# One store of 127 rows issued as two stores, of 112 and of 15 rows, in a fused attention, gating and Fourier kernel on Trainium2

## The chip, the cores and the metric

The kernel runs on one core of one Trainium2 chip. The metric is the device time of one execution in microseconds (us); of several runs the median is given. TensorE is called PE below, VectorE DVE, ScalarE ACT, GpSimd POOL and SyncE SP. SP computes nothing here: it is the queue from which almost all DMAs are issued, in program order.

## The reference

Three stages run one after the other, for a batch of 4, a sequence of 576 and a width of 512:

```python
# 1: attention in a window of 64 positions, 8 heads of 64
attn = softmax(where(0 <= i - j < 64, q @ k.T / 8, -1e9)) @ v
# 2: gated unit with a spatial mix
h = relu(x @ w_in); u, v = h[..., :512], h[..., 512:]
x = (u * (w_spatial @ layernorm(v) + b_spatial)) @ w_out
# 3: Fourier mix and channel MLP
u = x + real(fft(fft(x, axis=1), axis=2))
out = u + relu(layernorm(u) @ w_ch1) @ w_ch2
```

The change touches the end of the Fourier mix, where `u` of stage 3 is written to memory.

## The kernel before

Stages 1 and 2 and the Fourier mix run batch by batch (b = 0 to 3). Stage 3's channel MLP runs after them over all 2304 rows in five chunks of 384 or 512 rows (`TILES`, `GROUPS`). Numbers of 32 bits are split into a high and a low part, and a product is three matmuls (`PASS`).

The order of the work is written out by hand. A string for each batch (`ORDER`, lines 38 to 46) names the next step by a letter, and every engine runs its instructions in the order in which the steps issued them. While batch b goes through stage 2 and the Fourier mix (letters i and u, the `items` of line 675), the attention of batch b + 1 is woven in (letters s, q, v: attention step, load of q and k, load of v). In batch 3 there is no attention left; there the weights of the channel MLP are loaded and decoded (letter n) and the first chunk is loaded back and normalized (letters c and d). SP is one queue: a load that stands behind a store in the program is issued behind it.

The Fourier mix of a batch uses the symmetry of a real transform. `e2(b, mt)` (line 621) makes three tiles, mt = 0, 1 and 2. For mt = 0 and 1 it makes two tiles of `u`, r = 0 with rows in natural order and r = 1 with mirrored rows, and for mt = 2 one tile of 65 rows. A tile is written by DVE (lines 655 to 661) and finished by POOL (line 662), and then SP stores it to the scratch tensor `u_scr` in memory (lines 664 to 670). For mt = 0 and r = 1 row 0 would repeat a row that is already there, so only rows 1 to 127 are stored: 127 rows of 2 KB each. So each batch has one store of 128 rows (line 666), one of 127 (line 668), one of 128 (line 666), one of 128 (line 670) and one of 65 (line 664), in this order on SP, and the kernel has the 127-row store four times, at 147.7, 243.4, 332.2 and 417.3 us.

What stands behind these stores:

- In batch 0, SP next loads v for the attention (line 350). POOL shifts a copy of it (lines 355 and 356), and behind that on POOL stand the `norm_rstd` steps (lines 484 and 485) of the gating of batch 1.
- In batch 2, SP next loads two tiles `uu` of the first chunk back from `u_scr` (`load_u`, line 742) and then raw weights (line 218). DVE takes the statistics of the first tile (line 478), and behind that on DVE stand the normalizations (line 489) of the gating of batch 3. ACT splits their results (line 205), and then evacuates the `ps_u` results (line 533) that PE waits for before its next `ps_v` matmuls (line 500).
- In batch 3, the tile `u` of mt = 2 takes the buffer of an earlier tile `u` (the pool `tr` has five buffers), so DVE's line 655 waits until the store of that tile has landed. Behind it on DVE stands line 792, which makes the low part of the first hidden tile, and PE's second-layer matmuls (line 812) wait for that.

Of the kernel before, what the change touches and what calls it, by code (L numbers as in the profile page):

```python
# [111 lines left out]
def tile_kernel(ctx: ExitStack, tc: tile.TileContext, q, k, v, w_in, w_sp, b_sp, w_out, w_c1, w_c2,  # L112
                rows, ident, mask, t1h, t1l, s2c, s2s, out):
    nc = tc.nc
    act, dve, pool, pe, sp = nc.scalar, nc.vector, nc.gpsimd, nc.tensor, nc.sync
# [5 lines left out]
    def raw_tile(i):  # L121
        return st_p.tile([128, 512], I64, tag=f"st{i}", name="st")
# [16 lines left out]
    def psT(nm="psT"):  # L139
        return ps_t.tile([128, 512], F32, tag="t", name=nm)  # L140

    def psO(nm="psO"):
        return ps_o.tile([128, 512], F32, tag="o", name=nm)

    def tr(nm, shape=(128, 512), dt=F32):
        return tr_p.tile(list(shape), dt, tag="tr", name=nm)

    u_scr = dr_p.tile([B * S, DM], F32, name="u_scr")
# [472 lines left out]
    def e2(b, mt):  # L621
        rev, nat = REV[b], NAT[b] + mt * 128
        n = 128 if mt < 2 else 65
        cc = mt * 128
        xs = []
        for r in range(2 if mt < 2 else 1):
            px = psT("ps_xt")
            c0 = cc + 321 * r
            for m in range(4):
                pe.transpose(px[0:n, m * 128:(m + 1) * 128], FR[:, m, c0:c0 + n], idt)  # L630
            x = tr("x2h")
            act.activation(out=x[0:n], in_=px[0:n], func=AF.Copy, scale=0.5)
            xs.append(x)
        k = mt if b < B - 1 else 1 + mt
        if k < 2:
            room = raw_tile(k).bitcast(F32).rearrange("p (r d) -> p r d", r=2)
            room = [room[:, i] for i in range(2)]
        else:
            room = [tr("u") for _ in xs]
        pa, pb = psO("ps_a"), psO("ps_b")  # L640
        for ps, tb, c0, nn in ((pa, tc2, 0, NK2), (pb, ts2, 256, 256)):
            oc = slice(c0, c0 + nn)
            c = 0
            for kt in range(2):
                for w, a in PASS:
                    st = (2 * kt + w) * NM + cc
                    pe.matmul(ps[0:n, 0:nn], lhsT=tb[:, st:st + n], rhs=zz[:, kt, a, oc],
                              start=(c == 0), stop=False)
                    c += 1
            st = 4 * NM + cc  # L650
            pe.matmul(ps[0:n, 0:nn], lhsT=tb[0:99, st:st + n], rhs=zs[0:99, oc], start=False, stop=True)

        def row(r, x):
            u = room[r]
            dve.tensor_tensor(out=u[0:n, 0:257], in0=pa[0:n, 0:257], in1=x[0:n, 0:257], op=ALU.add)
            o = x[0:n, 257:512]
            if r == 0:
                dve.tensor_tensor(out=o, in0=o, in1=pb[0:n, 1:256], op=ALU.subtract)
            else:
                dve.tensor_tensor(out=o, in0=o, in1=pb[0:n, 1:256], op=ALU.add)  # L660
            dve.tensor_tensor(out=u[0:n, 511:256:-1], in0=u[0:n, 1:256], in1=o, op=ALU.subtract)
            pool.tensor_tensor(out=u[0:n, 1:256], in0=u[0:n, 1:256], in1=o, op=ALU.add)
            if mt == 2:
                sp.dma_start(out=u_scr[rev + 255:rev + 320, :], in_=u[0:65])
            elif r == 0:
                sp.dma_start(out=u_scr[nat:nat + 128, :], in_=u)
            elif mt == 0:
                sp.dma_start(out=u_scr[rev:rev + 127, :], in_=u[1:128])
            else:
                sp.dma_start(out=u_scr[rev + 127:rev + 255, :], in_=u)  # L670

        for r, x in enumerate(xs):
            row(r, x)
# [299 lines left out]
```

## Time and profile before

| what | value |
|---|---|
| time, median of 3 runs (lowest to highest) | 839.21 us (839.21 to 840.34) |
| time of the profiled execution | 839.83 us |
| its span in the trace | 838.0 us |
| mean granted clock of PE | 0.983 of full |
| PE busy (matmul) | 797.2 us, 95% of the span |
| DVE, ACT, POOL busy | 418.0, 316.0, 243.3 us |
| DMA on SP's queue | 55.23 MB, 23.6% of 16 engines over the span |

An engine's busy time is the time in which it ran instructions. The time around the span is 839.83 - 838.0 = 1.8 us. PE waits little as a whole; the waits that are left lie in few places, so single stretches have to be read and not the average.

### The profile page before, as it was taken

The numbers are of one execution on the slowest core, as the hardware profiler recorded it, in microseconds if no ns is written. First come the engines' busy times: TensorE is split into PE (matmuls) and PEld (weight loads), VectorE is DVE, ScalarE is ACT, GpSimd is POOL, SyncE is SP. The second block draws the span as 40 slices with busy tenths as digits, with TensorE's granted clock in tenths as the row PEclk, the third lists the DMA queues.
The fourth block names the chain that finished last, engine by engine and source line by source line (L and its number), as shares of the span: only waits on it lengthen the run. The fifth ranks groups of instructions, "written<-read, shape, count | busy, mean of one in ns | idle before, by whom it ended". The sixth has DMA issues, their size and how long they took to land.

```text
span 838.0 us, 13450 instructions
## 1 busy us (share of the span) xinstructions
PE 797.2 (95%) x4969; PEld 700.9 (84%) x4969; DVE 418.0 (50%) x1099; ACT 316.0 (38%) x939; POOL 243.3 (29%) x332
## 2 busy tenths in 40 slices
PE   6789999999999999797959999999999999999998
PEld 4678989889998999697959999988888888888886
DVE  3896766444463446376638888953212212231012
ACT  5877657365654554243413333321111111111100
POOL 2665552454224541345113333422000100000000
PEclk9999999999999999898979999999999999999999
DMA  8735433312222110423014444333000300011001
GB/s 202 176 84 171 126 102 93 99 33 60 54 61 68 31 26 16 142 81 97 14 44 151 128 126 139 110 93 122 13 13 14 101 12 26 14 51 50 1 1 50
DMA packets 89438, 62.71 MB, mean 75 GB/s; under 512 B 64859, under 2 KB 77403, under 8 KB 89373
## 3 DMA queue, kind: packets, MB, share of 16 engines
q1 hardware_dynamic: 87676, 55.23, 23.6%
q0 software_dynamic: 1696, 6.63, 2.3%
q8 instruction: 39, 0.64, 0.3%
q14 instruction: 27, 0.21, 0.1%
HBM read 52.40 MB, written 9.44 MB: 74 GB/s over the span
## 4 chain that ended last, share of the span: by engine, by line
PE 85%; DMA 5%; DVE 5%; issue 2%; POOL 1%; ACT 1%; SPq 1%; POOLq 0%; DVEq 0%; ACTq 0%
PE ps_y L812 24%; PE ps_h L788 24%; PE ps_v L500 6%; PE ps_d L558 6%; PE ps_u L530 5%; PE ps_c L543 5%; PE psS L389 3%; PE ps_x L443 3%; PE ps_pt L426 2%; PE ps_z L604 1%; DMA u_scr<-u 1%; DMA st<-in_moe_w_ch_dram 1%; PE ps_z L612 1%; DMA va<-in_v_dram 1%; PE ps_kn L366 1%
## 5 line engine op out<-in xcount | busy, mean ns | idle before, releaser
L812 PE MATMUL ps_y<-ar 128*128 128x512 f32 x756 | 184.1, 391 | 0.0
L812 PEld LDWEIGHTS ps_y<-ar 128*128 128x128 f32 x756 | 141.3, 188 | 28.2
L792 DVE SCALAR_TENSOR_TENSOR ar<-ps_h,ar 128x512 fp32r<-128x512 f32 (+1 forms) x80 | 50.9, 637 | 203.5 <-ACT ar L791 203.5
L791 ACT ACTIVATE ar<-ps_h 128x512 fp32r<-128x512 f32 (+1 forms) x80 | 44.4, 555 | 284.2 <-PE ps_h L788 284.2
L788 PE MATMUL ps_h<-ar 128*128 128x384 f32 (+1 forms) x672 | 147.9, 365 | 0.1
L788 PEld LDWEIGHTS ps_h<-ar 128*128 128x128 f32 x672 | 122.2, 188 | 16.8 <-issue 0.7
L207 POOL TENSOR_TENSOR ar<-dec,ar 128x512 fp32r<-128x512 f32 x36 | 49.7, 1382 | 69.0 <-ACT ar L205 68.7
L500 PE MATMUL ps_v<-ar 128*128 128x512 f32 (+1 forms) x240 | 61.1, 411 | 5.4 <-ACT uf L533 3.8
L402 ACT ACTIVATE P<-P,nm 128x128 f32<-128x128 f32 (+1 forms) x144 | 55.5, 386 | 17.1 <-DVE nm L396 12.3
L484 POOL TENSOR_SCALAR rs<-mv 128x1 f32<-128x1 f32 (+1 forms) x38 | 9.4, 247 | 180.6 <-DVE mv L479 180.2
L543 PE MATMUL ps_c<-ar 128*128 128x288 f32 x384 | 58.4, 302 | 1.2 <-DVE gf L548 1.2
L500 PEld LDWEIGHTS ps_v<-ar 128*128 128x128 f32 (+1 forms) x240 | 44.1, 187 | 18.3 <-ACT uf L533 4.1
L396 DVE CUSTOM_DVE_ANT_0 P<-psS,msk 128x128 f32<-128x128 f32 (+1 forms) x144 | 38.4, 268 | 41.8 <-PE psS L389 40.4
L558 PE MATMUL ps_d<-ar 128*128 128x288 f32 x384 | 54.7, 300 | 1.6 <-ACT qbd L373 1.6
L530 PE MATMUL ps_u<-ar 128*128 128x288 f32 x384 | 54.3, 297 | 1.3 <-ACT qbd L373 1.0
L543 PEld LDWEIGHTS ps_c<-ar 128*128 128x128 f32 x384 | 53.6, 193 | 1.5 <-DVE gf L548 1.4
L558 PEld LDWEIGHTS ps_d<-ar 128*128 128x128 f32 x384 | 51.9, 191 | 1.9 <-ACT qbd L373 1.9
L530 PEld LDWEIGHTS ps_u<-ar 128*128 128x128 f32 x384 | 51.4, 188 | 2.1 <-ACT qbd L373 1.2
L389 PE MATMUL psS<-kT,qbd 128*128 128x128 f32 (+1 forms) x288 | 45.1, 297 | 0.0
L788 PE MATMUL ps_h<-un,ar 128*128 128x512 f32 x168 | 44.0, 397 | 0.0
L418 POOL TENSOR_TENSOR P<-P,r 128x384 f32<-128x384 f32 x32 | 26.8, 838 | 49.6 <-ACT P L402 18.8
L389 PEld LDWEIGHTS psS<-kT,qbd 128*128 128x128 f32 x288 | 39.7, 209 | 0.1
(144 smaller groups left out, 1278.1 us busy)
## 6 DMA issues: line engine op xcount, KB each, us to landing
st<-in_moe_w_ch_dram SPq DMA_DIRECT2D x20, 512.0 KB, 3.7
uu<-u_scr SPq DMA_DIRECT2D x30, 256.0 KB, 2.7
uf<-in_moe_w_ch_dram SPq DMA_DIRECT2D x12, 512.0 KB, 3.8
va<-in_v_dram SPq DMA_DIRECT2D x40, 128.0 KB, 2.8
qn<-in_q_dram SPq DMA_DIRECT2D x48, 96.0 KB, 2.7
kn<-in_k_dram SPq DMA_DIRECT2D x36, 96.0 KB, 3.2
u_scr<-st SPq DMA_DIRECT2D x10, 256.0 KB, 5.6
uf<-in_moe_w_in_dram SPq DMA_DIRECT2D x4, 512.0 KB, 5.6
```

The costliest lines, as they stand in the source:

```text
L207: (lo_eng or pool).tensor_tensor(out=lo, in0=x, in1=hi.bitcast(F32), op=ALU.subtract)
L389: pe.matmul(ps[:, j, 0:n], lhsT=qbd[:, s % 2, j].rearrange("p h c -> p (h c)"), rhs=w, start=True, stop=True)
L396: dve.tensor_tensor_reduce(out=P[:, j, 0:n], in0=ps[:, j, 0:n], in1=msk[:, 128 - n:128], scale=1.0, scalar=3.0e38, op0=ALU.add, op1=ALU.mi ...
L402: act.activation(out=P[:, j, 0:n], in_=P[:, j, 0:n], func=AF.Exp, scale=-1.0, bias=nm[:, j:j + 1], accum_out=sm[:, j:j + 1])
L500: pe.matmul(pf[0:n], lhsT=xt[:, kt, a, m * 128:m * 128 + n], rhs=wi[:, 4:8, kt, w], start=(c == 0), stop=(c == 11))
L530: pe.matmul(ps[:, 0:HS], lhsT=wi[:, f, kt, w], rhs=xt[:, kt, a, t], start=(c == 0), stop=(c == 11))
L543: pe.matmul(ps[:, 0:HS], lhsT=vn[:, m, a, dd], rhs=ws[:, m, w, t], start=(c == 0), stop=False)
L558: pe.matmul(ps[:, 0:HS], lhsT=wo[:, kt, w, m * 128:(m + 1) * 128], rhs=G[:, kt, a, t], start=(c == 0), stop=(c == 11))
L788: pe.matmul(ps[:, 0:n_t], lhsT=w[:, 0, a, kt * 128:(kt + 1) * 128], rhs=un[kt][:, x, :], start=(n == 0), stop=(n == 11))
L791: act.activation(out=h[:, 0], in_=ps[:, 0:n_t], func=AF.Relu)
L792: dve.scalar_tensor_tensor(out=h[:, 1], in0=ps[:, 0:n_t], scalar=0.0, in1=h[:, 0].bitcast(F32), op0=ALU.max, op1=ALU.subtract)
L812: pe.matmul(acc[i], lhsT=h[:, a, cc], rhs=w[:, 1, x], start=(j == 0 and z == 0), stop=(j == NFF - 1 and z == 2))
```

## The change

In each batch the store of 127 rows is issued as two stores one behind the other on SP: the first 112 rows and the last 15. Source, destination and bytes are the same as before.

```diff
             elif mt == 0:
-                sp.dma_start(out=u_scr[rev:rev + 127, :], in_=u[1:128])
+                sp.dma_start(out=u_scr[rev:rev + 112, :], in_=u[1:113])
+                sp.dma_start(out=u_scr[rev + 112:rev + 127, :], in_=u[113:128])
             else:
                 sp.dma_start(out=u_scr[rev + 127:rev + 255, :], in_=u)
```

## Rows read from the trace of the kernel before

**Rows 1.** The page: busy time, share and instructions of each engine.

```profile
PE 797.2 (95%) x4969; PEld 700.9 (84%) x4969; DVE 418.0 (50%) x1099; ACT 316.0 (38%) x939; POOL 243.3 (29%) x332
```

**Rows 2.** Chain that ended last, in order of time: start, length, what.

```profile
174.75 5.54 PE ps_v L500 x24
...
347.96 6.65 DMA st<-in_moe_w_ch_dram
355.08 7.43 PE ps_v L500 x24
...
419.54 11.05 DMA u_scr<-u
```

**Rows 3.** SP's queue in order of time, batch 3: start, time in issue, line, operation.

```profile
417.33 0.24 SPq L668 DMA_DIRECT2D u_scr<-st  x1
419.54 2.00 SPq L666 DMA_DIRECT2D u_scr<-u  x1
421.69 0.46 SPq L670 DMA_DIRECT2D u_scr<-u  x1
```

**Rows 4.** Table by stretches: length, busy time by engine, granted clock, DMA share, GB/s.

```profile
174.00:174.40 0.40, 0.40 (x10) 0.33 (x9) 0.40 (x5) 0.34 (x2) 0.00 (x0) 1.00 0.93 209
...
417.00:418.00 1.00, 1.00 (x11) 1.00 (x10) 0.66 (x2) 0.00 (x0) 0.31 (x1) 1.00 0.74 262
...
429.00:430.00 1.00, 0.00 (x0) 0.00 (x0) 0.00 (x0) 0.00 (x0) 0.00 (x0) 0.50 0.07 27
...
433.50:434.00 0.50, 0.50 (x3) 0.40 (x2) 0.50 (x1) 0.00 (x0) 0.49 (x1) 0.50 0.64 172
```

**Rows 5.** Issue and landing of line 666's first store, batch 0; the page's DMA issues.

```profile
L666 SPq DMA_DIRECT2D u_scr<-st x1: 355/355/355, 146.6 to 146.6; - x1
...
DMA to landing us min/median/max: 2.0/2.0/2.0
...
uu<-u_scr SPq DMA_DIRECT2D x30, 256.0 KB, 2.7
...
u_scr<-st SPq DMA_DIRECT2D x10, 256.0 KB, 5.6
```

**Rows 6.** Instructions in order of time, batch 3's end; in brackets idle time before.

```profile
421.69 0.60 ACT L632 ACTIVATE x2h<-ps_xt 65x512 f32<-65x512 f32 x1 [4.90 <-POOL u L662]
...
430.70 0.42 DVE L655 TENSOR_TENSOR u<-ps_a,x2h 65x257 f32<-65x257 f32 x1 [9.95 <-DMA u_scr<-u]
...
431.83 1.01 DVE L792 SCALAR_TENSOR_TENSOR ar<-ps_h,ar 128x384 fp32r<-128x384 f32 x2
...
432.43 3.35 PE L812 MATMUL ps_y<-a,ar 128*128 128x512 f32 x7 [8.75 <-DVE ar L792]
```

**Rows 7.** Table by stretches as in group 4: the first 5 us after that wait.

```profile
432.40:437.40 5.00, 4.97 (x14) 4.30 (x15) 3.69 (x5) 0.09 (x1) 1.59 (x2) 0.53 0.09 27
```

**Rows 8.** Instructions in order of time, SP, DVE and PE, beginning of batch 3.

```profile
338.30 0.33 SPq L742 DMA_DIRECT2D uu<-u_scr  x1
...
342.68 6.47 PE L530 MATMUL ps_u<-ar 128*128 128x288 f32 x48
...
347.20 0.70 DVE L478 BATCH_NORM_STATS2 bn<-uu 128x6 f32<-128x512 f32 x1 [4.78 <-DMA uu<-u_scr]
...
350.59 0.66 PE L771 MATMUL ps_un<-idt,uu 128*128 128x128 f32 x4 [1.43 <-DVE uu L489]
...
355.08 7.41 PE L500 MATMUL ps_v<-ar 128*128 128x512 f32 x24 [3.84 <-ACT uf L533]
```

**Rows 9.** Instructions in order of time, PE, later in batch 3.

```profile
381.59 1.84 PE L543 MATMUL ps_c<-ar 128*128 128x288 f32 x12 [1.21 <-DVE gf L548]
...
387.07 1.11 PE L771 MATMUL ps_un<-idt,uu 128*128 128x128 f32 x4 [3.37 <-DVE uu L489]
```

**Rows 10.** POOL's wait after batch 0's store.

```profile
162.61 0.40 POOL L355 TENSOR_SCALAR vb<-va 64x256 f32<-64x256 f32 x1 [8.04 <-DMA va<-in_v_dram]
```

**Rows 11.** Table by stretches as in group 4, after the stores of batches 0 and 1.

```profile
162.00:170.00 8.00, 6.37 (x52) 5.51 (x52) 3.69 (x15) 3.50 (x11) 6.36 (x11) 1.00 0.23 52
240.00:270.00 30.00, 30.00 (x222) 26.58 (x221) 14.78 (x56) 14.12 (x44) 14.33 (x22) 1.00 0.31 84
```

## The prediction, made before the changed kernel was run

> **What bounds the kernel now.** I read the busy times first: PE is busy for 95% of the span [rows 1], so only a place where PE stands still can give much. The chain of work that ended last says where that is. It is PE nearly throughout, and two of its long pieces that are not PE lie close behind a 127-row store: 6.65 us on weight loads at 348 and 11.05 us on a store `u_scr<-u` at 419.5 [rows 2].
>
> The second one is not a 127-row store. It is line 666's store of 128 rows, issued 2.2 us behind one [rows 3]. The same kind of store alone takes 0.36 us to issue and lands after 2.0 us [rows 5]. Here it took 2.00 us to issue [rows 3] and 11.05 to land. So I looked at what the DMA engines did in that time. Beside a 128-row store they are busy to 0.74 and move 262 GB/s, but at 429 us they are busy to 0.07 and move 27 GB/s [rows 4]. A share of 0.07 of 16 engines is about one engine. 127 rows of 2 KB are 260 KB, and 260 KB at 27 GB/s take 9.6 us. So **the 127-row store goes through one engine for some 10 us**, and whatever else has a piece on that engine lands behind it. This is a reading of a sum over the engines; no row gives the engine of a packet.
>
> **What becomes of the store.** The question is how 112 and 15 rows are spread. No row shows either count. The nearest to 112 are the loads of 96 rows of q and k, during which, at 174.0 us, the share is 0.93 [rows 4]; the nearest to 15 is the 65-row store, alone at 433.5 us with a share of 0.64 and 172 GB/s [rows 4]. Both are spread over many engines, and neither is a power of two or a full tile. I take the 112 rows as spread like the 128-row store, landing after 2.0 us [rows 5]. For the 15 rows the bounds are next to nothing if they are spread, and 31 KB at 27 GB/s = 1.1 us if they sit on one engine. For the pair the other end is today's 10 us.
>
> [...]
>
> **The cost added.** Four more issues on SP. The 127-row issue takes 0.24 us [rows 3], one that is spread 0.36 [rows 5], so each batch adds about 2 x 0.36 - 0.24 = 0.5 us on SP. In batch 3 SP stands idle from 417.6 to 419.5 us, waiting for POOL's tile [rows 3], which hides it; and the next store's issue gets 1.6 us shorter, if it is the busy engine that holds it. I cost it at nothing; with no cover it would be 4 x 0.5 = 2 us.
>
> **Batch 3 (419 to 437 us).** DVE's line 655 waits 9.95 us for that store and starts at 430.70; line 792 follows at 431.83 behind it on DVE, and PE resumes at 432.43 after 8.75 us of nothing [rows 6]. After: the store lands at 419.54 + 2.0 = 421.5. The next thing that is late is ACT's line 632, which waits for POOL and not for a DMA and ends at 421.69 + 0.60 = 422.3 [rows 6]. So DVE starts line 655 at about 422.35, 8.35 us earlier, and PE resumes at 424.1, after 0.4 us of idling. ACT's next tile waits for line 670's store, issued at 421.69 [rows 3]; at 2.0 us it lands at 423.7, in time.
>
> There is a second gain. [...] With PE hardly stopped that work takes 5.0 x 0.53 = 2.65 us: 2.35 us less. Together **10.7 us**. If only the idle time goes, it is 8.4; if the landing takes 5.6 us, the median of the stores that now stand in the queue [rows 5], line 655 starts at 425.2 and 5.5 us are won before any clock.
>
> **Batch 2 (332 to 362 us).** DVE's statistics on the reloaded tile `uu` wait 4.78 us until 347.20 [rows 8]. The load was issued at 338.30 [rows 8]; the median of such loads is 2.7 us [rows 5], so free of the busy engine it lands at 341.0, and DVE is free for it at 347.20 - 4.78 = 342.42. Everything behind it on DVE, then POOL and ACT, moves up by 4.78 us, and with it the end of PE's wait for ACT's line 533: 355.08 becomes 350.30. PE's own work before that ends at 342.68 + 6.47 = 349.15, and the transposes of 0.66 us fit in the gap [rows 8]; half a microsecond of idling is left. The weight loads that the chain names [rows 2] stand on SP behind the second `uu` load; they start some 8 us earlier as well, and ACT needs them only behind line 533. The matmuls that follow took 7.43 us at 355.08 against 5.54 for the same 24 in batch 1 [rows 2]; that is the clock again, 1.89 us. Together **6.7 us**; 4.8 if the clock falls anyway.
>
> **Batch 0 (154 to 170 us).** POOL waits 8.04 us for v [rows 10], and PE, covered by gating matmuls until 162, then idles 8.00 - 6.37 = 1.63 us in pieces, at a clock of 1.00 [rows 11]. With v landing like the `uu` loads, in some 2.7 us [rows 5] where it took over 8, POOL's steps run some 5 us earlier, under those matmuls: **1.6 us**, between 0.8 and 1.63.
>
> **Batch 1.** PE is busy for 30.00 of 30.00 us around the store [rows 11]. Nothing, and that is also what hides the extra issue there.
>
> **Sum.** 10.7 + 6.7 + 1.6 = 19.0 us. From the profiled execution's 839.83 that leaves 820.8; it ran 0.62 us above the median of 839.21, so for a median I say 820.2.
>
> **The rivals.**
>
> *The gain of batch 2 is given back.* Further on in batch 3 PE waits again, 1.21 us and 3.37 us, for DVE [rows 9], with weights and the first chunk's rows in DVE's queue. If that work were paced by something else, by transfers for instance, PE would only reach it sooner and wait longer. Against it: SP issues those loads when DVE has freed a buffer, and DVE's steps there stand behind PE's `ps_v`, so all of it should move up together. Then 820.2 + 6.7 = 826.9. The opposite, that these waits shrink too, would give up to 4.6 us more: 815.6.
>
> *A slow landing in batch 3.* At 5.6 us PE would idle 3.3 us, and the clock might fall as it did after 3.84 us in batch 2 [rows 8]: the 10.7 becomes about 5.5, and the time 825.4. For it stands only that median; against it, that it is made up of stores behind the busy engine.
>
> *The change does not do what it says.* What makes the store slow may be not the count of rows but that it starts at row 1 of its tile, as the 112 rows still do. Then the pair takes the same 10 us on one engine: 839.2. The rows can't exclude it, since only the 127-row store starts there.
>
> [...]
>
> *Slower: the 15 rows become the slow store.* They begin at row 113, and if that made them slow on one engine, they would take the place of the 127. It turns from gain to loss where they land later than today's stall ends: some 13 us for 15 rows, 0.87 us a row, against 2 KB at 27 GB/s = 0.076 us. At 1 us a row all three waits grow by some 2 us, to about 845. Nothing in the trace is so slow.
>
> **How the numbers follow.** Forecast 0.78, the giving back 0.07, its opposite 0.04, slow landing 0.06, no effect 0.03, slower 0.02. The likeliest case gives 820.2. Its own bounds are 839.2 - 19.0 with the clock terms missing (4.2) and 0.8 less in batch 0: 825.2 at most; with the giving back and the slow landing the range reaches to 827, and with smaller waits later to 816. A measurement of this kernel can tell about 0.2%, 1.7 us, from no change: faster 0.95, same 0.03, slower 0.02.
>
> **What would show it.** Right: line 666's second store in each batch issued in about 0.36 us and landed in 2 to 3; no stretch at 27 GB/s; DVE's line 655 at the end of batch 3 waiting for ACT, PE's gap there under 1 us and the clock at 1.00; the statistics of `uu` unwaited; PE full from 162 to 170. Wrong: a stretch of share 0.07 behind the stores, or PE's waits at 381 and 387 grown by what batch 2 saved.

## The result and the profile after

The changed kernel takes 818.29 us (median of 4 runs, 817.22 to 819.24) beside 839.78 us for the kernel before on the same chip (839.21 to 840.71): a ratio of 0.9743, with a 95% interval of 0.9726 to 0.976, or 21.5 us less. The forecast was 820.2 us, 19.0 us less. The profiled execution took 817.22 us, its span is 815.4 us; it is the fastest of the four, so the gain in the ledger below, 22.6 us, is about 1 us more than the medians give. Lines behind the change are numbered one higher.

The page of the changed kernel, busy times and one row of its DMA issues:

```profile
PE 791.6 (97%) x4969; PEld 696.9 (85%) x4969; DVE 418.4 (51%) x1099; ACT 315.9 (39%) x939; POOL 243.5 (30%) x332
...
u_scr<-st SPq DMA_DIRECT2D x10, 256.0 KB, 2.2
```

The instructions are the same and so is the work of DVE, ACT and POOL [rows 1]; PE's busy time fell by 5.6 us, and its mean granted clock over the span rose from 0.983 to 0.996. The stores of 128 rows now land after a median of 2.2 us where it was 5.6 [rows 5].

SP's queue at the end of batch 3, which answers to [rows 3]:

```profile
405.52 0.32 SPq L668 DMA_DIRECT2D u_scr<-st  x1
405.90 0.43 SPq L669 DMA_DIRECT2D u_scr<-st  x1
407.74 0.34 SPq L666 DMA_DIRECT2D u_scr<-u  x1
409.90 0.34 SPq L671 DMA_DIRECT2D u_scr<-u  x1
```

The two parts take 0.32 and 0.43 us to issue, and SP is still done more than a microsecond before the next tile is ready. That tile's store takes 0.34 us to issue instead of 2.00. The 15-row store, all four of them, issue and landing in the changed kernel:

```profile
L669 SPq DMA_DIRECT2D u_scr<-st x4: 427/428/431, 146.9 to 405.9; - x4
...
DMA to landing us min/median/max: 1.9/2.0/2.0
```

The profile has no landing for the 112-row store. The DMA share while it moves, together with the 15 rows behind it, answers to [rows 4]:

```profile
406.20:407.20 1.00, 1.00 (x10) 1.00 (x9) 0.51 (x2) 0.00 (x0) 0.23 (x1) 1.00 0.79 250
```

The same rows that moved at 27 GB/s now move at 250, about as the 128 rows do (262 [rows 4]).

The instructions around the wait of batch 3, which answer to [rows 6]:

```profile
409.91 0.59 ACT L632 ACTIVATE x2h<-ps_xt 65x512 f32<-65x512 f32 x1 [4.92 <-POOL u L662]
...
410.53 0.42 DVE L655 TENSOR_TENSOR u<-ps_a,x2h 65x257 f32<-65x257 f32 x1 [1.57 <-ACT x2h L632]
...
411.65 1.01 DVE L793 SCALAR_TENSOR_TENSOR ar<-ps_h,ar 128x384 fp32r<-128x384 f32 x2
...
412.26 1.90 PE L813 MATMUL ps_y<-a,ar 128*128 128x512 f32 x7 [0.40 <-DVE ar L793]
```

DVE waits 1.57 us for ACT where it waited 9.95 us for a DMA, and PE waits 0.40 us where it waited 8.75.

Three stretches of the changed kernel in the table by stretches (length, busy time of PE, PEld, DVE, ACT and POOL, granted clock, DMA share, GB/s), from the top: after batch 0's stores, after PE's wait behind batch 2's store, and after the wait in batch 3. The first answers to the first row of [rows 11], the last to [rows 7].

```profile
156.00:170.00 14.00, 14.00 (x107) 12.77 (x105) 5.55 (x22) 7.39 (x22) 7.87 (x11) 1.00 0.19 42
...
346.50:352.00 5.50, 5.42 (x24) 3.79 (x25) 3.75 (x8) 3.14 (x8) 1.68 (x3) 1.00 0.02 4
412.20:417.20 5.00, 4.94 (x24) 4.45 (x25) 3.97 (x7) 1.84 (x4) 1.80 (x2) 1.00 0.09 27
```

The clock is 1.00 in all three, and PE goes through 24 matmuls in the 5 us in which it did 14 before [rows 7]. Batch 2 and 3 in the changed kernel, in order of time: the load of the `uu` tiles, the statistics on the first one, and PE's waits, which answer to [rows 8, 9].

```profile
332.61 1.90 SPq L743 DMA_DIRECT2D uu<-u_scr  x2
...
338.63 0.68 DVE L478 BATCH_NORM_STATS2 bn<-uu 128x6 f32<-128x512 f32 x1
...
338.98 6.48 PE L530 MATMUL ps_u<-ar 128*128 128x288 f32 x48
...
346.57 5.80 PE L500 MATMUL ps_v<-ar 128*128 128x512 f32 x24 [0.69 <-ACT uf L533]
...
370.97 1.87 PE L543 MATMUL ps_c<-ar 128*128 128x288 f32 x12 [0.65 <-DVE gf L548]
...
376.45 1.11 PE L772 MATMUL ps_un<-idt,uu 128*128 128x128 f32 x4 [3.35 <-DVE uu L489]
```

The statistics start with no wait, 6.0 us behind the load's issue, and PE's wait for line 533 shrinks from 3.84 to 0.69 us; the wait of 1.43 us for the transposes is gone. In batch 0, POOL's wait for v [rows 10] became:

```profile
155.42 0.40 POOL L355 TENSOR_SCALAR vb<-va 64x256 f32<-64x256 f32 x1 [2.08 <-DMA va<-in_v_dram]
```

**The ledger.** Each line compares the start of the same piece of PE's or SP's work in the two profiled executions; what is new in the difference belongs to the stretch before it.

| up to | before | after | difference | of which new |
|---|---|---|---|---|
| first store of batch 0 | 146.6 | 145.3 | 1.2 | 1.2 |
| PE's 24 `ps_v` matmuls of batch 1 | 174.75 | 171.04 | 3.7 | 2.5 |
| PE's `ps_u` matmuls of batch 3 | 342.68 | 338.98 | 3.7 | 0.0 |
| PE's 24 `ps_v` matmuls of batch 3 | 355.08 | 346.57 | 8.5 | 4.8 |
| PE's transposes behind the 3.35 us wait | 387.07 | 376.45 | 10.6 | 2.1 |
| batch 3's 127-row store | 417.33 | 405.52 | 11.8 | 1.2 |
| PE's resumption at line 812 | 432.43 | 412.26 | 20.2 | 8.4 |
| end of the span | 838.0 | 815.4 | 22.6 | 2.4 |

### The profile page after: what moved, and what is told of

Read it like the earlier page. It is cut to its first block, busy times and chain, and to the rows that moved or that the text cites. A ratio compares the mean times of both kernels' runs of the same rounds, so it can differ in the third digit from the quotient of the medians.

```text
span 815.4 us, 13454 instructions
## 1 busy us (share of the span) xinstructions
PE 791.6 (97%) x4969; PEld 696.9 (85%) x4969; DVE 418.4 (51%) x1099; ACT 315.9 (39%) x939; POOL 243.5 (30%) x332
## 4 chain that ended last, share of the span: by engine, by line
PE 88%; DVE 6%; issue 2%; DMA 1%; POOL 1%; ACT 1%; SPq 1%; POOLq 0%; ACTq 0%; DVEq 0%
PE ps_y L813 24%; PE ps_h L789 24%; PE ps_v L500 6%; PE ps_d L558 6%; PE ps_c L543 5%; PE ps_u L530 4%; PE psS L389 3%; PE ps_x L443 3%; PE ps_pt L426 2%; PE ps_z L604 2%; PE ps_z L612 1%; PE ps_un L772 1%; PE ps_kn L366 1%; PE ps_qn L371 1%; PE ps_xt L630 1%
## 5 line engine op out<-in xcount | busy, mean ns | idle before, releaser
L500 PE MATMUL ps_v<-ar 128*128 128x512 f32 (+1 forms) x240 | 59.4, 403 | 2.3 <-DVE ar L447 1.6
```

The source lines that it names most:

```text
L500: pe.matmul(pf[0:n], lhsT=xt[:, kt, a, m * 128:m * 128 + n], rhs=wi[:, 4:8, kt, w], start=(c == 0), stop=(c == 11))
```

## The experiments

Two questions were open: whether the count of rows is what spreads a store, and whether the ledger's parts are each caused by the store of their own batch. The first three runs cut the 127 rows elsewhere, the fourth sends them from another queue; the rest apply the split in one batch only.

**113 and 14 rows.** The same as the change, one row further on:

```diff
-                sp.dma_start(out=u_scr[rev:rev + 127, :], in_=u[1:128])
+                sp.dma_start(out=u_scr[rev:rev + 113, :], in_=u[1:114])
+                sp.dma_start(out=u_scr[rev + 113:rev + 127, :], in_=u[114:128])
```

> The same split as the change, one row further on: 113 rows and 14 rows. [...] A stretch of DMA share 0.07 at 27 GB/s is back behind the stores. [...] Rival B (any cut into two stores does it, or the 127 rows were slow for their start at row 1 and 15 rows less cure it): as the change, 818 us.

It took 834.77 us beside 838.72, a ratio of 0.9963 (0.9945 to 0.9982): 3.1 us less (1.5 to 4.6), where the change gave 21.5. The ratio is taken over all executions, so here and below the gain that follows from it is not quite the difference of the two medians, which is 4.0 us here. In this kernel, a stretch of the table, and PE's waits behind the stores of batches 2 and 3:

```profile
423.00:424.00 1.00, 0.00 (x0) 0.00 (x0) 0.00 (x0) 0.00 (x0) 0.00 (x0) 0.50 0.07 27
```

```profile
347.16 0.66 PE L772 MATMUL ps_un<-idt,uu 128*128 128x128 f32 x4 [0.45 <-DVE uu L489]
...
427.48 2.93 PE L813 MATMUL ps_y<-a,ar 128*128 128x512 f32 x6 [7.76 <-DVE ar L793]
```

The stretch of one engine's share is back, and PE's wait is 7.76 us, just 1.0 less than before. So it is neither the cut itself nor the start at row 1 of the tile: the first store starts there in both kernels, and one row more in it gives most of the gain back. The time came out 1.2 us below the 836 to 839 us that were estimated. That range had only the store's 1.0 us to go by (113 x 2 KB at 27 GB/s are 8.6 us, 127 rows 9.6), but it came in at more than one place: PE's wait of 1.43 us in batch 2 [rows 8] fell to 0.45 as well, and of PE's three waits in batch 0 the two short ones, 0.35 and 0.30 us, are gone.

**118 and 9 rows.**

```diff
-                sp.dma_start(out=u_scr[rev:rev + 127, :], in_=u[1:128])
+                sp.dma_start(out=u_scr[rev:rev + 118, :], in_=u[1:119])
+                sp.dma_start(out=u_scr[rev + 118:rev + 127, :], in_=u[119:128])
```

> Split into 118 rows and 9 rows. [...] In batch 3 the store of line 666 lands some 3 us later than with the change and PE idles about 3 us instead of 0.4, with or without a fall of the clock (0 to 2 us more); batch 2 and batch 0 lose nothing, since what waits there has more slack than 3 us: 820 to 824 us. Rival B: as the change, 818 us. [...]

It took 823.94 us, a ratio of 0.9827 (0.9788 to 0.9866). A stretch of the table within the wait, and the wait itself:

```profile
415.50:416.50 1.00, 0.06 (x1) 0.00 (x0) 0.00 (x0) 0.12 (x1) 0.00 (x0) 1.00 0.13 51
```

```profile
418.99 1.19 PE L813 MATMUL ps_y<-a,ar 128*128 128x512 f32 x4 [3.44 <-DVE ar L793]
```

The share is 0.13 at 51 GB/s, twice that of one engine, and PE waits 3.44 us, between the 0.40 with 112 rows and the 7.76 with 113. The expected 3 us go back to an estimate: 118 x 2 KB at twice 27 GB/s are 4.5 us. So 118 rows move at the share of two engines, and that is much better than the share of one.

**126 and 1 row.**

```diff
-                sp.dma_start(out=u_scr[rev:rev + 127, :], in_=u[1:128])
+                sp.dma_start(out=u_scr[rev:rev + 126, :], in_=u[1:127])
+                sp.dma_start(out=u_scr[rev + 126:rev + 127, :], in_=u[127:128])
```

> Split into 126 rows and a single row. [...] A rival by which it is the multiple of 16 in 112 that counts: 126 rows sit on one or two engines, 820 to 838 us.

It took 817.78 us, a ratio of 0.9754 (0.9724 to 0.9785); the time of the change, 817 to 820 us, was expected. The stretch in which the 126 rows move, and PE's wait at the end of batch 3:

```profile
409.30:410.30 1.00, 1.00 (x10) 1.00 (x9) 0.44 (x2) 0.00 (x0) 0.30 (x1) 1.00 0.78 240
```

```profile
415.26 1.89 PE L813 MATMUL ps_y<-a,ar 128*128 128x512 f32 x7 [0.37 <-DVE ar L793]
```

The share is 0.78 and PE waits 0.37 us, as with 112 rows. The multiple of 16 is not needed.

**127 rows from POOL's queue.**

```diff
-                sp.dma_start(out=u_scr[rev:rev + 127, :], in_=u[1:128])
+                pool.dma_start(out=u_scr[rev:rev + 127, :], in_=u[1:128])
```

> The 127 rows in one store as before, but issued by POOL and not by SP. If it is spread over many engines from there: as the change, 817 to 821 us, with no stretch of share 0.07. [...]

It took 818.58 us, a ratio of 0.9768 (0.9734 to 0.9802), the same as the change. The stretch after the store's issue at 407.31 us, and issue and landing of the four stores:

```profile
408.50:409.50 1.00, 1.00 (x9) 1.00 (x7) 0.33 (x1) 0.00 (x0) 0.63 (x1) 1.00 0.83 244
```

```profile
L668 POOL DMA_DIRECT2D u_scr<-st x4: 609/612/623, 146.6 to 407.3; - x4
...
DMA to landing us min/median/max: 2.8/3.2/4.6
```

From POOL the same 127 rows in one store move at a share of 0.83 and 244 GB/s and land in 3.2 us. So 127 rows move at one engine's share from SP's queue and at that of many from POOL's.

**The split in one batch at a time.** Four kernels, with b = 3, 2, 0 and 1 in the condition:

```diff
             elif mt == 0:
-                sp.dma_start(out=u_scr[rev:rev + 127, :], in_=u[1:128])
+                if b == 3:
+                    sp.dma_start(out=u_scr[rev:rev + 112, :], in_=u[1:113])
+                    sp.dma_start(out=u_scr[rev + 112:rev + 127, :], in_=u[113:128])
+                else:
+                    sp.dma_start(out=u_scr[rev:rev + 127, :], in_=u[1:128])
```

> The split in batch 3 alone, the other three stores as before. By the ledger of the prediction this is 10.7 us of the gain (8.35 us of PE's wait and some 2.1 to 2.35 us of clock): 828 to 829.5 us beside 839. A rival by which the wait in batch 3 comes from stores queued up since earlier batches: less than 8 us. The time of the first store of batch 0 in its profile, 146.6 before and 145.3 with the change, is a control: nothing of the change lies before it, so it should move by a us or so either way from run to run.

> The split in batch 2 alone. By the ledger 6.4 to 6.7 us (4.8 of DVE's wait for the reloaded tile, 1.6 to 1.9 of clock): 832.5 us beside 839. In the profile of the change another 1.7 us were won between 368 and 395, where PE waits for DVE; if batch 2's store is the cause of that too, 830.5 to 831. A rival by which the gain of batch 2 is given back at those waits: 837 to 839.

> The split in batch 0 alone. By the prediction 1.6 us; by the profile of the change 2.5 us, since each of PE's waits there costs more than the idle time that the profile shows. 836.5 to 837.5 us beside 839. A rival by which PE's waits after 162 us were not v's doing: no difference.

> The split in batch 1 alone. PE is busy without a gap around that store before and after: no difference from 839, within 0.2% (1.7 us). A rival by which the extra issue on SP costs something wherever it isn't paid back: 839.5 to 841.

The gain is worked out from each ratio and 838 us; the kernel before had a median of 837.75 us here (11 executions):

| split in | time, us | ratio (interval) | gain, us | expected gain |
|---|---|---|---|---|
| batch 3 | 829.42 | 0.9894 (0.9876 to 0.9912) | 8.9 (7.4 to 10.4) | 10.7 |
| batch 2 | 831.13 | 0.9922 (0.9903 to 0.9941) | 6.5 (4.9 to 8.1) | 6.4 to 6.7 |
| batch 0 | 834.89 | 0.9971 (0.9947 to 0.9994) | 2.4 (0.5 to 4.4) | 1.6 to 2.5 |
| batch 1 | 838.45 | 1.0004 (0.9982 to 1.0025) | -0.3 (-2.1 to 1.5) | 0 |

PE's waits behind the stores of batches 2 and 3, first with the split in batch 3 alone, then with the split in batch 2 alone (lines behind the edit are numbered four higher than in the kernel before):

```profile
351.53 0.66 PE L775 MATMUL ps_un<-idt,uu 128*128 128x128 f32 x4 [1.45 <-DVE uu L489]
...
356.03 7.25 PE L500 MATMUL ps_v<-ar 128*128 128x512 f32 x24 [3.84 <-ACT uf L533]
...
424.48 1.90 PE L816 MATMUL ps_y<-a,ar 128*128 128x512 f32 x7 [0.40 <-DVE ar L796]
```

```profile
351.46 5.82 PE L500 MATMUL ps_v<-ar 128*128 128x512 f32 x24 [0.68 <-ACT uf L533]
...
424.60 3.29 PE L816 MATMUL ps_y<-a,ar 128*128 128x512 f32 x7 [8.78 <-DVE ar L796]
```

With the split in batch 0 alone, PE from 156 to 170 us:

```profile
156.00:170.00 14.00, 14.00 (x103) 12.81 (x103) 5.92 (x21) 6.98 (x21) 8.14 (x12) 1.00 0.21 47
```

Each split takes away the waits behind the store of its own batch and leaves those behind the others: with batch 2 alone the wait of 8.78 us in batch 3 is untouched, with batch 3 alone PE's two waits behind batch 2's store, 1.45 and 3.84 us, are. Batch 1 gives nothing, and the extra issue on SP costs nothing that can be measured there. The four gains add up to 17.5 us against 21.5 for all together. The intervals allow that, if only just: the kernel before itself had a median of 837.75 us beside these four and 839.78 beside the change, and an error in the former goes into all four gains. Batch 3 alone came out lower than expected, with an interval that ends just below 10.7; in its profile PE resumes 8.4 us earlier, measured from batch 3's first store, and the rest of the span is 2.1 us shorter, together 10.5. Whether that or the 8.9 is nearer the truth is left open.

## Why the prediction was right

**The reading of the store** held. One engine's share of 0.07 was taken for 127 rows on one engine; the runs with 113, 118 and 126 rows put it to the test, and 0.07, 0.13 and no such stretch came out. The engines are still seen only through the share, as in the prediction. What bears the reading is that PE's wait at the end of batch 3 goes with the share: 8.75 and 7.76 us at 0.07 with 127 and 113 rows, 3.44 at 0.13 with 118, 0.40 and 0.37 at 0.79 and 0.78 with 112 and 126, and 0.28 at 0.83 with 127 rows from POOL's queue. Why a count of rows moves at one share and not at another was not shown; nor is it the count alone, as POOL's queue shows.

**Batch 3** was forecast at 8.35 us of waiting and 2.35 of clock. The ledger has 8.4, and 2.4 for all that follows. The 2.35 is an estimate that scales the 5.0 us of [rows 7] by their granted clock of 0.53; no run shows that term by itself, and what the changed kernel showed in its place is a clock of 1.00 and 24 matmuls in 5 us instead of 14. The step that named what is late next was right to the letter: DVE waits for ACT's line 632, and PE idles 0.4 us.

**Batch 2** was forecast at 4.78 us of waiting and 1.89 of clock. The ledger has 4.8, and the 24 matmuls behind it took 1.6 us less, at a granted clock of 1.00 where it was 0.76. The chain of the changed kernel, which answers to [rows 2], has 5.82 us instead of 7.43, and still 0.28 more than for the same matmuls in batch 1:

```profile
171.04 5.54 PE ps_v L500 x24
...
346.57 5.82 PE ps_v L500 x24
```

**Batch 1 and the added cost** were forecast at nothing, and nothing was found.

**Batch 0** was mis-sized: 1.6 us forecast and 1.63 at most, 2.5 in the ledger, 2.4 (0.5 to 4.4) when split alone. The term counted only the idle time that the profile shows. PE's rows in the kernel before and in the changed one, in order of time:

```profile
163.81 0.52 PE L426 MATMUL ps_pt<-idt,P 128*64 128x128 f32 x3
164.09 1.82 PE L530 MATMUL ps_u<-ar 128*128 128x288 f32 x12
166.21 1.84 PE L530 MATMUL ps_u<-ar 128*128 128x288 f32 x12 [0.30 <-ACT vr L504]
169.03 3.58 PE L530 MATMUL ps_u<-ar 128*128 128x288 f32 x24 [0.98 <-ACT qbd L373]
```

```profile
162.25 6.64 PE L530 MATMUL ps_u<-ar 128*128 128x288 f32 x48
```

In three pieces the 48 matmuls show 1.82 + 1.84 + 3.58 = 7.24 us of busy time, in one piece 6.64. The two interruptions cost 0.6 us beside the 1.28 of idle time that stands in the brackets. The first two rows show a likely reason: where PE goes on without a stop, a piece of work starts before the row ahead of it has ended, at 164.09 against 163.81 + 0.52 = 164.33. If each of the two interruptions cost such an overlap of 0.24 us, that would be 0.5 of the 0.6 us; this is an estimate from these two rows, and no run shows it.

**What was not forecast.** The ledger has 1.2 us ahead of the first changed instruction. Among the ten profiled kernels of this case the first store of batch 0 starts anywhere from 145.0 to 148.0 us, with the same instructions ahead of it, so this is chance. Further, 1.7 us were won between the 24 matmuls of batch 3 and its 127-row store: 0.5 in PE's two waits for DVE [rows 9], and 1.2 behind them. For the latter, which is a matter of the clock, here are the 10 us behind the second wait in the kernel before, in the changed one, with the split in batch 3 alone, with 126 and 1 row, and with the split in batch 2 alone, one fence each:

```profile
387.00:397.00 10.00, 9.93 (x57) 9.94 (x58) 4.28 (x10) 3.80 (x11) 4.74 (x7) 0.71 0.19 54
```

```profile
376.40:386.40 10.00, 9.95 (x67) 9.95 (x68) 5.23 (x11) 4.27 (x13) 4.94 (x8) 0.85 0.26 79
```

```profile
387.30:397.30 10.00, 9.96 (x57) 9.97 (x58) 4.14 (x9) 3.77 (x11) 4.76 (x7) 0.70 0.18 56
```

```profile
378.20:388.20 10.00, 9.92 (x57) 9.93 (x58) 4.27 (x10) 3.82 (x11) 4.75 (x7) 0.71 0.20 57
```

```profile
381.70:391.70 10.00, 9.97 (x77) 9.98 (x78) 5.66 (x12) 4.60 (x14) 5.63 (x9) 1.00 0.27 79
```

The two waits and the clock behind them, for all ten profiled kernels, ordered by what batch 2's store was:

| kernel | batch 2's store | the two waits, us | granted clock, next 10 us |
|---|---|---|---|
| before | 127 rows, SP | 1.21, 3.37 | 0.71 |
| split in batch 3 alone | 127 rows, SP | 0.64, 3.35 | 0.70 |
| split in batch 0 alone | 127 rows, SP | 2.25, 2.83 | 0.69 |
| split in batch 1 alone | 127 rows, SP | 0.92, 3.37 | 0.71 |
| 113 and 14 | 113 and 14, SP | 0.95, 3.36 | 0.83 |
| 118 and 9 | 118 and 9, SP | 2.05, 3.36 | 0.84 |
| 126 and 1 | 126 and 1, SP | 1.94, 2.51 | 0.71 |
| 127 rows from POOL | 127 rows, POOL | 2.05, 3.37 | 0.83 |
| split in batch 2 alone | 112 and 15, SP | 1.02, 3.35 | 1.00 |
| the change | 112 and 15, SP | 0.65, 3.35 | 0.85 |

The waits together are between 4.0 and 5.4 us, 4.6 in the kernel before, and both ends occur with the whole gain of batch 2 in hand. So neither the rival by which they grow by what batch 2 saved, 6.7 us, nor the one by which they go, 4.6 us, came true. The clock behind them is another matter. With the whole store on SP in batch 2 it is 0.69 to 0.71 in all four kernels; of the other six, five have 0.83 to 1.00 and one, with 126 rows, has 0.71. The kernel with 113 rows has the higher clock although PE's wait of 3.8 us behind batch 2's store is still there. One profile of each kernel can't tell whether the clock goes with batch 2's store or changes from execution to execution, so it stays open whether these 1.2 us belong to the change. Taking the 1.2 us of chance off the 22.6 leaves 21.4 for the change, and without the 1.7 us as well 19.7, beside the 19.0 of the sum. The 21.5 us of the result have a like uncertainty: the four executions of the kernel before lie at 839.21 us and above, while 24 later ones have medians of 838.72 and 837.75, and beside the former the cut at 126 rows gains 20.6 us by its ratio.

**The other rivals.** The slow landing did not come: the stores of 128 rows land in 2.2 us, so the median of 5.6 was that of 2.0, 2.0, 9.2 and 11.9 us, of which the two long ones are stores behind the 127 rows. That rival's second step, a fall of the clock behind 3.3 us of idling, didn't have to follow either: with 118 rows PE waited 3.44 us at that place, and the clock of the next 5 us stayed at 1.00:

```profile
418.90:423.90 5.00, 4.91 (x24) 4.44 (x25) 4.15 (x7) 0.99 (x3) 1.68 (x2) 1.00 0.09 27
```

That the start at row 1 makes the store slow is refuted by the pair of 112 and 113 rows. The 15 rows land in 2.0 us, so they are not the slow store.

## What to carry to other kernels

Look at the row count of the stores on SP's queue: here 127 and 113 rows moved at the share of one engine, 118 at that of two, and 112, 126 or a full 128 at that of many, and at one engine's 27 GB/s the 260 KB of 127 rows take some 10 us. The loss did not show at the slow store but at its neighbours: in batch 3 a store of 128 rows issued just behind it landed after 11.05 us instead of 2.0 [rows 2, 5], and DVE, which waits for it, has the wait in the profile. A stretch where every engine is idle and the DMA share stands at 0.07, a sixteenth, is the sign that showed it in this trace; moving the one store to POOL's queue (818.58 us) served as well as cutting it (818.29).

## What was not expected

SP's issues just behind the slow store took long, but not each time. In batches 0, 1 and 2 of the kernel before, one of the two issues behind it took 3.22, 2.70 and 2.78 us, where in the changed kernel none of the same issues took more than 1.06. In batch 3 the next issue took 2.00 us in the kernel before [rows 3], but 0.33 in the three kernels that have the same store there and the split in batch 0, 1 or 2 alone. The first such issue of the kernel before, and the one in batch 3 with the split in batch 1 alone:

```profile
149.08 3.22 SPq L666 DMA_DIRECT2D u_scr<-st  x1
```

```profile
420.75 0.33 SPq L666 DMA_DIRECT2D u_scr<-u  x1
```

PE's wait at the end of batch 3 is 8.8 us either way, so it is the late landing that costs the time and not the issue; what decides how long the issue takes was not found.

And the clock behind one and the same place, a wait of 2.5 to 3.4 us for DVE, lay between 0.69 and 1.00 over 10 us from profile to profile, which is up to 3 us of PE's time. A difference of that size between two single profiles must not be put down to the edit without more executions.
